# Two row pairs instead of one at each pass's end of a gated feed-forward block

## The chip, the cores and the metric

The kernel runs on one core of one Trainium2 chip. The metric is device time in microseconds of one execution; lower is better. Before the change the median of three runs is 1755.19 us (1753.89 to 1756.28).

## The reference: what is computed

One transformer block with an adaptive layer norm. Six vectors of 512 (shift, scale and gate for each half) come from a small product with a condition vector. The first half is attention: 2048 query rows, 32 heads of 128 that share 8 key and value heads, over the last 512 cached positions. The second half, where the change lies, is a gated feed-forward net with inner width 1792:

```
h = _layernorm(x) * (1 + cb) + sb
x = x + gb * ((_gelu(h @ w_gate) * (h @ w_up)) @ w_down)
```

Everything is float32 outside; x is 2048 x 512.

## The kernel before, in words

*Precision.* Each float32 operand is split into a high and a low float16 half, and a product is three matmuls of 128x128 by 128x512 (low by high, high by high, high by low), summed in one bank of PSUM. All go through the helper at line 89.

*Attention* takes most of the time. It is written as a list of 512 steps whose order on every engine is fixed by hand. In its second half the feed-forward weights are prepared between its steps: scaled, combined, split and stored in device memory under keys (tiles `stage`, `kept`), by `prep_set` for gate and up and by `prep_wd` for the down weights.

*The feed-forward part* goes twice over the inner width, once for each half of the 2048 rows (a pass). A pass has seven pairs n of two f-tiles (NP = 7, so n runs from 0 to 13 over both passes). For each pair there are two matrices, q = 2n (gate) and q = 2n + 1 (up), 28 in all. A matrix is a 2x2 block product by seven products instead of eight (Winograd's form of Strassen); the loop at the end of the kernel walks its seven products in the order 1, 2, 6, 7, 5, 4, 3. Each is six matmuls, and each is called a step here; it has the index k from 0 to 6. The sums go to banks of the names fa, fb, fc. ACT copies some of them out (fg, fu, u; line 884), DVE adds the others (line 1269), ACT applies the GELU with a scale (line 1275), DVE multiplies gate by up (line 1286), and ACT and DVE or POOL split the result into the halves `at` (lines 1296 and 1297).

*The down product* of a pair comes in two kinds, told apart by `turned(n)`:
- By rows (`y_tasks`): for each of the eight row tiles, two f-tiles, six matmuls. The bank is `py`, and DVE adds it to the row tile `acc` (line 951). 48 matmuls a pair.
- Turned (`yt_tasks`): seven products in each of two halves p of the model width, on four combinations of the activations that POOL makes (`sums_of`, lines 1302 and 1297). 42 matmuls a pair. The output is transposed: DVE adds each product into eight tiles `yt` of 128 columns by 512 rows (line 1655, or 1658 for the first).

Before, six of the seven pairs of a pass are turned and the last is by rows. At the end of a pass the eight `yt` tiles are turned back: ACT splits each into its upper and lower 16-bit parts (`yu`, line 1664), a transposing DMA on SP's queue writes `yv` (line 1669), ACT puts the parts together to rows `yr` (line 1685), and POOL adds them to `acc` (line 1686), which holds the first half's result reloaded from device memory. Then the row tile goes out (`f_final`).

*What sets the order.* Products of the down kind wait in a list `nexty`; `y_next` takes the first entry and issues it. `put_off(n, fn)` runs fn n steps later (`tick` counts one at each step). In the feed-forward part this order is the program's order; on PE, DVE, ACT and POOL a planner with its own costs sets the final order, taking the earliest instruction in the program that its model finds ready. SP's queue, which issues all these DMAs, stays in the order written: weight fetches for the next matrices (`set_fetch`, `wd_fetch`), the transposes, row loads and output stores stand behind one another.

*Buffers.* Tiles of one kind share a number of buffers: `p16` four (the splits yu, and fu, the up-matrix's first copy), `qt` three, `raw` five, `acc` eight (the `yt` tiles and the row tiles share them), `ot` twelve (the halves `at`), and five PSUM banks `acc` beside one `qa` and two `s`.

Of the kernel before, what the change touches and what calls it, by code (L numbers as in the profile page):

```python
# [12 lines left out]
U16 = mybir.dt.uint16  # L13
BF16 = mybir.dt.bfloat16
AF = mybir.ActivationFunctionType
ALU = mybir.AluOpType
AX = mybir.AxisListType

P = 128
# [3 lines left out]
KT = D // P  # L23
NF = F // P
NT = S // P
QB = 512
QT = QB // P
# [17 lines left out]
NRAW = 5  # L45
NRW = 2
NWR = 2
GW = 3
NACC = 5
NP16 = 4  # L50
# [13 lines left out]
def block_kernel(ctx: ExitStack, tc: tile.TileContext, x, kT, v, wq, wo, wg, wu, wd, cT, wc, wm, out):  # L64
    nc = tc.nc

    const = ctx.enter_context(tc.tile_pool(name="const", bufs=1))
    pool = ctx.enter_context(tc.tile_pool(name="pool", bufs=2))
# [7 lines left out]
    def raw(name):  # L76
        return pool.tile([P, 512], F32, tag="raw", name=name, bufs=NRAW)
# [13 lines left out]
    acc, moved, bg = {}, [0], []  # L91
# [9 lines left out]
    def rows_of(t, i):  # L101
        return t[i * P:(i + 1) * P, :]
# [188 lines left out]

    def turned(n):

        return n % NP < NP - 1

    def f_spread(i, m):
        w = little("lw", 1, 2)
# [157 lines left out]
    def put_off(n, fn):  # L455

        waits_.append([n, fn])
# [137 lines left out]
    for g in range(NG):  # L595
        half, pr = divmod(g, NPR)
        for j, qb in (PLAIN if g < GW else TURNED):
            units.append((half, pr, 2 * half + qb, 2 * pr + j))
# [194 lines left out]
    def set_steps(key, by, act=False):  # L793
        l, r = slice(0, 256), slice(256, 512)

        def tt(o, a, b, op):
            nc.gpsimd.tensor_tensor(o, a, b, op=op)

        def s0():
            SET[key] = [get_w(0)]  # L800
            times(RAW[key][0], by)
            halves(SET[key][0], RAW[key][0], act)

        def s1():
            r1 = RAW[key][1]
            times(r1, by)
            SET[key] += [None, None, pool.tile([P, 2, 256], F16, tag="x3", name="x3", bufs=2)]
            halves(SET[key][3], r1[:, r], act)
            tt(r1[:, r], r1[:, l], r1[:, r], ALU.add)

        def s2():
            r0, r1 = RAW[key][0], RAW[key][1]
            tt(r1[:, l], r0[:, l], r1[:, l], ALU.subtract)
            tt(r0[:, l], r1[:, r], r0[:, l], ALU.subtract)
            tt(r0[:, r], r0[:, r], r0[:, l], ALU.subtract)

        def s3():
            SET[key][1] = get_w(1)
            halves(SET[key][1], RAW[key][0], act)

        def s4():
            SET[key][2] = get_w(2)
            halves(SET[key][2], RAW[key].pop(1), act)

        return s0, s1, s2, s3, s4
# [22 lines left out]
    def sched_set(key, srcs, t0, by, spread):  # L848
        s0, s1, s2, s3, s4 = set_steps(key, by)
        a, b, c, d, e, f = SETPOS2 if key == GW else SETPOS  # L850
        sched_pair(key, srcs, t0 - a, spread, [(t0 - b, s0), (t0 - e, s3)], [(t0 - c, s1), (t0 - d, s2), (t0 - f, s4)])
# [357 lines left out]
    for g in range(NG):  # L1209
# [5 lines left out]
        spread = None if half else lambda m, pr=pr: w_spread(pr, m)  # L1215
        if 0 < g < GW:
            a, b = plain_steps(g, by)
            sched_pair(g, srcs, t0 - (19 if g > 1 else 13), spread, [(t0 - (13 if g > 1 else 8), a)], [(t0 - (11 if g > 1 else 7), b)])
        elif g >= GW and (not half or pr < GW):
            sched_set(g, srcs, t0, by, spread)  # L1220
            if not half:
                a, b, c, d, e, f = SETPOS2 if g == GW else SETPOS
                for k, pos in ((0, t0 - b + 4), (3, t0 - c + 4), (1, t0 - e + 4), (2, t0 - f + 4)):
# [27 lines left out]
    NP = NF // 2  # L1251
    NQ = 4 * NP
# [134 lines left out]
    def prep_wd(n, b):  # L1387
# [4 lines left out]
        def load(k):  # L1392
            st[k] = pool.tile([P, D], F32, tag="wr", name="wr", bufs=NWR)
            dma(st[k], wd[(2 * n + k) * P:(2 * n + k + 1) * P, :])
# [72 lines left out]
    loads.sort(key=lambda l: l[0])  # L1467
    released = {"raw": [0] * NRAW, "rw": [0] * NRW, "wr": [0] * NWR}
    for pos, (load, steps), kind, ahead in loads:
# [38 lines left out]
    def pushes(u, y):  # L1508
        g, k = divmod(u, 4)
        pv = pv_tasks(u - 2) if 2 <= u < NU + 2 else []  # L1510
        if u >= NU:
# [6 lines left out]
            return []  # L1518
        nxt = items(g + 1) if g + 1 >= GW else None
        if g < GW:  # L1520
# [14 lines left out]
    with tc.manual_schedule():  # L1535
        begin()
        nexty, invs = [], {}
        for t in range(T + TAIL):
            now[0] = t
            u, s = divmod(t, 4)  # L1540
# [65 lines left out]
    def y_next():  # L1606
        if nexty:
            all_of(nexty.pop(0))
# [15 lines left out]
    for i in range(2 * QT):  # L1624
        q = 7 * (2 + i // 2) + 3 * (i % 2)
        load, norm, split, turn = ln_turned(i)
# [6 lines left out]
    for p in range(2):  # L1633
        q = 51 + 14 * p
# [4 lines left out]

    def f_final(ti):  # L1640
        assert ti in back
        if ti not in halfway:
            return halfway.add(ti)
        if ti >= 2 * QT:
            dma(rows_of(out, ti), acc[ti])
        else:
            put_off(2, lambda: dma(rows_of(out, ti), acc[ti]))

    YT, YR, back, halfway = {}, {}, set(), set()

    def yt_add(n, c, qb, ps):
        by = ST["dyc"][:, KT * (n % NP) + c:KT * (n % NP) + c + 1]
# [7 lines left out]
    def yt_turn(g, c, qb):  # L1660

        def split():
            u = YR["u", c, qb] = pool.tile([P, 2, QB], U16, tag="p16", name="yu", bufs=NP16)
            nc.scalar.activation(u, YT[g, c, qb].bitcast(U16).rearrange("p (r h) -> p h r", h=2), AF.Copy)

        def turn():
            if ("t", qb) not in YR:
                YR["t", qb] = pool.tile([P, KT, 2 * QT, P], U16, tag="pt", name="yv", bufs=NPT)
            nc.sync.dma_start_transpose(YR["t", qb][:, c], YR.pop(("u", c, qb)).rearrange("p a b -> p (a b)"))

        split()
        put_off(2, turn)
        YR["n"] = YR.get("n", 0) + 1
        if YR["n"] % QT == 0:
            for i in range(QT):
                ti = 2 * QT * g + (YR["n"] - 1) % (2 * QT) // QT * QT + i
                put_off(3, lambda ti=ti: load_acc(ti, y1[ti]) or back.add(ti))

    def yt_rows(g, qb):
        t = YR.pop(("t", qb)).rearrange("p c (h i) q -> p c q h i", h=2)  # L1680
        for i in range(QT):
            ti = 2 * QT * g + QT * qb + i
            assert ti in back
            r = raw("yr")
            nc.scalar.activation(r.bitcast(U16).rearrange("p (c q h) -> p c q h", c=KT, h=2), t[:, :, :, :, i], AF.Copy)
            nc.gpsimd.tensor_tensor(acc[ti], acc[ti], r, op=ALU.add)
            f_final(ti)

    ADDS = {1: ((0, 0),), 2: ((0, 0),), 6: ((0, 1),), 5: ((1, 1),), 7: ((1, 1),), 4: ((1, 0),), 3: ((0, 1),)}
    YORDER = (1, 2, 6, 5, 7, 3, 4)  # L1690
    LAST = {2: (0, 0), 7: (1, 1), 3: (0, 1), 4: (1, 0)}

    def yt_tasks(n):
        tasks = []
        for p in range(2):
            st = {}
            bk = banks(st, {"a": ("acc", "ya", NACC) if p else ("qa", "ya", 1), "b": ("acc", "yb", NACC), "c": ("acc", "yc", NACC)})

            def group(k, p=p, bk=bk):
                a, b = PROD[k]  # L1700
                x, start = CHAIN[k]
                ci, off = YCOL[a]
                w, t = WO["f", n, ci], A[n, {"b11": "11", "b21": "21", "b22": "22"}.get(b, b)]
                sl = slice(off + p * P, off + (p + 1) * P)
                mm3(bk(x)(), w[:, 0, sl], w[:, 1, sl], t[:, 0, :], t[:, 1, :], start, k in (2, 4, 3), True)

            def post(k, p=p, st=st):
                (i, qb), = ADDS[k]
                yt_add(n, 2 * i + p, qb, st[CHAIN[k][0]])
                if n % NP == NP - 2 and k in LAST:  # L1710
                    i, qb = LAST[k]
                    c, g = 2 * i + p, n // NP
                    put_off(1, lambda: yt_turn(g, c, qb))
                    if p and k in (3, 4):
                        put_off(7 if g else 9, lambda: yt_rows(g, qb))

            tasks += [[(lambda k=k, f=group: f(k), lambda k=k, f=post: f(k))] for k in YORDER]
        return tasks

    YCOL = {"a11": (0, 0), "a12": (0, 256), "s2": (1, 0), "s3": (1, 256), "s4": (2, 0), "s1": (2, 256), "a22": (3, 0)}  # L1720

# [1 line left out]
    for q in range(NQ):  # L1723
        n, m = divmod(q, 2)
        its = items(NG + q) if q < 2 else f_items(q)
        for k, pk in enumerate(ORDER):
            if (q, pk) not in f_done:
                all_of(its[pk])
            run(("f", q, k))
            tick()  # L1730
            if n and k == 2 and m == 0 and turned(n - 1):
                nexty += yt_tasks(n - 1)
            if k in ((1, 2, 5, 6) if q < NQ - 1 else (1, 5)) or (n and turned(n - 1)):
                y_next()
            if q == NQ - 2 and k > 1 or (q, k) in ((NQ - 1, 1), (NQ - 1, 2)):
                y_next()
        if m == 1 and not turned(n):
            for qi, (a, b) in enumerate((("11", "21"), ("12", "22"))):
                for i in range(QT):
                    nexty.append(y_tasks((2 * (n // NP) + qi) * QT + i, [lambda n=n, a=a: A[n, a], lambda n=n, b=b: A[n, b]],  # L1740
                                         [("f", n, 0), ("f", n, 1)], col("dysc", n % NP), f_final))
# [40 lines left out]
```

## Time and profile before

| | us |
|---|---|
| median of three runs | 1755.19 |
| profiled execution | 1756.2 |
| its span, first to last instruction | 1754.4 |
| PE busy | 1713.0 (98%) |
| DVE busy | 1424.3 (81%) |
| ACT busy | 1263.0 (72%) |
| POOL busy | 1069.8 (61%) |

A row of a group gives line, engine, operation, output and inputs, shape and count, then the busy time, the mean in ns and the idle time of the engine before them with what ended it. A row of waits gives who waited for whom, the total, how often, and the longest. A row of the timeline gives start, duration, engine, what, and in brackets the idle time before. Busy times of PE overlap, since matmuls are pipelined: one is shown with some 380 ns, and the next one starts 216 ns after it.

### The profile page before, as it was taken

How to read it: one execution, taken by the hardware profiler on the slowest of the kernel's cores; microseconds unless marked ns; L12 is line 12 of the kernel's file. 1: busy time of each engine (PE TensorE's matmuls, PEld its weight loads, DVE VectorE, ACT ScalarE, POOL GpSimd, SP SyncE). 2: the span in 40 equal slices, each digit the busy share in tenths (PEclk: the TensorE clock that was granted, in tenths of full speed). 3: DMA queues.
4: the chain of work that ended last, by engine and by line, in shares of the span. 5: the costliest groups of instructions: out<-in, count | busy, mean ns of one | idle time of the engine just before them, and what ended most of it. 6: DMA issues, size and time to landing. Idle time of an engine off the chain costs nothing.

```text
span 1754.4 us, 26202 instructions
## 1 busy us (share of the span) xinstructions
PE 1713.0 (98%) x8008; PEld 785.4 (45%) x8010; DVE 1424.3 (81%) x2464; ACT 1263.0 (72%) x2819; POOL 1069.8 (61%) x1292
## 2 busy tenths in 40 slices
PE   7999999999999999999999999999999999999995
PEld 5444444444444444444444444444444444444442
DVE  7898898888888899888888888888885687747764
ACT  6988888888878777887778777787773744553334
POOL 4889777776888874655585585675511657243342
PEclk9999999999999999999999999999999999999998
DMA  7999999999999999999999999999985663463325
GB/s 236 217 206 210 212 215 210 223 206 219 222 209 235 202 210 178 216 208 235 202 213 230 215 212 212 205 220 218 204 169 146 190 190 105 117 208 117 100 84 150
DMA packets 691885, 341.01 MB, mean 194 GB/s; under 512 B 578976, under 2 KB 602272, under 8 KB 691744
## 3 DMA queue, kind: packets, MB, share of 16 engines
q1 hardware_dynamic: 691456, 338.81, 84.8%
q8 instruction: 63, 1.03, 0.3%
q14 instruction: 78, 0.64, 0.1%
q10 hardware_dynamic: 288, 0.52, 0.1%
HBM read 136.45 MB, written 62.26 MB: 113 GB/s over the span
## 4 chain that ended last, share of the span: by engine, by line
PE 81%; DVE 5%; ACT 5%; DMA 3%; POOL 3%; issue 2%; SPq 0%; DVEq 0%; POOLq 0%; ACTq 0%
PE py L89 18%; PE po L89 16%; PE ps L89 16%; PE qa L89 8%; PE fa L89 6%; PE qc L89 4%; PE fc L89 3%; PE ya L89 2%; PE qb L89 2%; PE fb L89 2%; PE yc L89 1%; DMA pt<-p 1%; ACT ee L990 1%; ACT p L1002 1%; PE pq L89 1%
## 5 line engine op out<-in xcount | busy, mean ns | idle before, releaser
L990 ACT ACTIVATE ee<-ps,nm 128x512 f32<-128x512 f32 x512 | 349.8, 683 | 191.9 <-DVE nm L981 188.2
L1007 DVE SCALAR_TENSOR_TENSOR p<-ee,rr,p 128x512 f16<-128x512 f32 x512 | 456.4, 891 | 5.0 <-ACT p L1002 4.2
L981 DVE TENSOR_REDUCE nm<-ps 128x1 f32<-128x512 f32 x512 | 350.4, 684 | 104.7 <-PE ps L89 101.9
L89 PE MATMUL ps<-k,qt 128*128 128x512 f16 x1536 | 415.1, 379 | 6.1 <-ACT ee L990 5.1
L1002 ACT ACTIVATE p<-ee,rr 128x512 f16<-128x512 f32 x512 | 364.4, 712 | 20.8 <-DVE rr L998 10.5
L89 PE MATMUL po<-pt,v 128*128 128x512 f16 x1536 | 373.1, 380 | 2.2 <-DMA pt<-p 2.1
L89 PE MATMUL py<-wo,ot 128*128 128x512 f16 x1536 | 371.5, 380 | 0.0
L89 PEld LDWEIGHTS <-w 128*128 128x128 f16 x2184 | 213.0, 98 | 267.2 <-issue 7.0
L89 PEld LDWEIGHTS <-v 128*128 128x128 f16 x1536 | 149.8, 98 | 184.6 <-issue 2.5
L89 PEld LDWEIGHTS <-ot 128*128 128x128 f16 x1536 | 150.1, 98 | 181.7 <-DVE ot L739 0.4
L89 PEld LDWEIGHTS <-qt 128*128 128x128 f16 x1536 | 145.8, 98 | 177.5 <-issue 4.6
L1302 POOL TENSOR_TENSOR fg<-fg 128x512 f32<-128x512 f32 x48 | 62.3, 1299 | 142.4 <-DVE fg L1286 141.4
L739 DVE SCALAR_TENSOR_TENSOR ot<-po,ot 128x512 f16<-128x512 f32 x128 | 87.7, 685 | 39.4 <-ACT ot L738 39.1
L1296 ACT ACTIVATE at<-fg 128x512 f16<-128x512 f32 x92 | 56.9, 625 | 66.8 <-DVE fg L1286 40.0
L990 ACT ACTIVATION_READ_ACCUMULATOR ee<-ps,nm 128x1 f32 x512 | 100.0, 195 | 0.0
L951 DVE SCALAR_TENSOR_TENSOR acc<-py,ysc,acc 128x512 f32<-128x512 f32 x128 | 94.7, 740 | 6.2 <-PE py L89 6.2
L234 POOL TENSOR_TENSOR lw<-lw,half__86 128x1 f32<-128x1 f32 x37 | 23.4, 631 | 104.9 <-DVE lw L184 104.8
L89 PE MATMUL fa<-t,w 128*128 128x512 f16 x336 | 82.7, 379 | 4.2 <-ACT u L884 2.2
L89 PE MATMUL qa<-t,w 128*128 128x512 f16 x348 | 84.9, 380 | 0.0
L396 POOL TENSOR_TENSOR rs<-rs,nhalf 128x1 f32<-128x1 f32 x32 | 18.7, 584 | 102.6 <-DVE rs L390 99.7
L1655 DVE SCALAR_TENSOR_TENSOR yt<-ya,dyc,yt 128x512 f32<-128x512 f32 x84 | 61.8, 745 | 23.9 <-PE ya L89 23.5
L89 PE MATMUL ya<-at,wo 128*128 128x512 f16 x288 | 77.5, 379 | 1.5 <-ACT at L1296 0.9
(241 smaller groups left out, 2802.3 us busy)
## 6 DMA issues: line engine op xcount, KB each, us to landing
w<-kept SPq DMA_DIRECT2D x123, 256.0 KB, 3.3
wo<-kept SPq DMA_DIRECT2D x72, 256.0 KB, 3.3
kept<-stage SPq DMA_DIRECT2D x62, 256.0 KB, 3.2
raw<-in_wo SPq DMA_DIRECT2D x56, 256.0 KB, 3.3
kept<-w SPq DMA_DIRECT2D x39, 256.0 KB, 3.5
rw<-in_wq SPq DMA_DIRECT2D x38, 256.0 KB, 3.2
hs<-hf SPq DMA_DIRECT2D x32, 256.0 KB, 2.8
pt<-p SPq DMA_TRANSPOSE x512, 3.5
```

The costliest lines, as they stand in the source:

```text
L89: nc.tensor.matmul(ps, a, b, start=first and n == 0, stop=last and n == 2, skip_group_check=chain)
L234: nc.gpsimd.tensor_tensor(out, out, half_, op=ALU.pow)
L396: nc.gpsimd.tensor_tensor(st["rs"], st["rs"], nhalf, op=ALU.pow)
L739: return lambda: nc.vector.scalar_tensor_tensor(t[:, 1, :], src, scale, t[:, 0, :], op0=ALU.mult, op1=ALU.subtract)
L951: nc.vector.scalar_tensor_tensor(acc[ti], st["p"], by, acc[ti], op0=ALU.mult, op1=ALU.add)
L981: nc.vector.tensor_reduce(nm, E[t]["ps"], axis=AX.X, op=ALU.max, negate=True)
L990: nc.scalar.activation(e, E[t]["ps"], AF.Exp, bias=E[t]["nm"], scale=1.0, accum_out=sm[:, t % 2:t % 2 + 1])
L1002: nc.scalar.activation(p16[:, 0, :], E[t]["e"], AF.Copy, scale=E[t]["r"])
L1007: nc.vector.scalar_tensor_tensor(p16[:, 1, :], E[t]["e"], E[t]["r"], p16[:, 0, :], op0=ALU.mult, op1=ALU.subtract)
L1296: nc.scalar.activation(t[:, 0, :], g, AF.Copy)
L1302: nc.gpsimd.tensor_tensor(g[o], g[a], g[b], op=ALU.subtract)
L1655: nc.vector.scalar_tensor_tensor(YT[key], ps, by, YT[key], op0=ALU.mult, op1=ALU.add)
```

## The change

`NROW = 2` pairs at each pass's end are by rows instead of one, so five of seven are turned. The preparation of the down weights follows `turned(n)`. The turned products are put into the list two by two, and taken at steps k = 1, 2, 5 and 6 alone, where before one was taken at every step (two at some steps of the last two matrices). Splits take buffers of the kind `qt` instead of `p16`; their transposes are issued three steps behind the split instead of two; the split of two of the eight tiles is put off one step more. The row copies and POOL's adds are put off one by one instead of four in one call: 9 to 12 steps after the last product for rows of the first block of 512, and 13 to 16 for the second, where before it was 9 (first pass) or 7 (second). A row tile is final after three contributions instead of two.

```diff
+NROW = 2
     def turned(n):
 
-        return n % NP < NP - 1
+        return n % NP < NP - NROW
...
     def f_final(ti):
         assert ti in back
-        if ti not in halfway:
-            return halfway.add(ti)
+        halfway[ti] = halfway.get(ti, 0) + 1
+        if halfway[ti] <= NROW:
+            return
...
-            u = YR["u", c, qb] = pool.tile([P, 2, QB], U16, tag="p16", name="yu", bufs=NP16)
+            u = YR["u", c, qb] = pool.tile([P, 2, QB], U16, tag="qt", name="yu", bufs=3)
...
-        put_off(2, turn)
+        put_off(3, turn)
...
-    def yt_rows(g, qb):
-        t = YR.pop(("t", qb)).rearrange("p c (h i) q -> p c q h i", h=2)
-        for i in range(QT):
-            ti = 2 * QT * g + QT * qb + i
-            assert ti in back
-            r = raw("yr")
-            nc.scalar.activation(r.bitcast(U16).rearrange("p (c q h) -> p c q h", c=KT, h=2), t[:, :, :, :, i], AF.Copy)
-            nc.gpsimd.tensor_tensor(acc[ti], acc[ti], r, op=ALU.add)
-            f_final(ti)
+    def yt_row(g, qb, i):
+        t = YR["t", qb].rearrange("p c (h i) q -> p c q h i", h=2)
+        ti = 2 * QT * g + QT * qb + i
+        assert ti in back
+        r = raw("yr")
+        nc.scalar.activation(r.bitcast(U16).rearrange("p (c q h) -> p c q h", c=KT, h=2), t[:, :, :, :, i], AF.Copy)
+        nc.gpsimd.tensor_tensor(acc[ti], acc[ti], r, op=ALU.add)
+        f_final(ti)
+        if i == QT - 1:
+            del YR["t", qb]
...
-                if n % NP == NP - 2 and k in LAST:
+                if n % NP == NP - NROW - 1 and k in LAST:
                     i, qb = LAST[k]
                     c, g = 2 * i + p, n // NP
-                    put_off(1, lambda: yt_turn(g, c, qb))
+                    put_off(2 if k in (3, 4) and p == k // 4 else 1, lambda: yt_turn(g, c, qb))
                     if p and k in (3, 4):
-                        put_off(7 if g else 9, lambda: yt_rows(g, qb))
-
-            tasks += [[(lambda k=k, f=group: f(k), lambda k=k, f=post: f(k))] for k in YORDER]
-        return tasks
+                        for r in range(QT):
+                            put_off((9 if k == 4 else 13) + r, lambda r=r: yt_row(g, qb, r))
+
+            tasks += [(lambda k=k, f=group: f(k), lambda k=k, f=post: f(k)) for k in YORDER]
+        return [tasks[k:k + 2] for k in range(0, len(tasks), 2)]
...
-            if k in ((1, 2, 5, 6) if q < NQ - 1 else (1, 5)) or (n and turned(n - 1)):
-                y_next()
-            if q == NQ - 2 and k > 1 or (q, k) in ((NQ - 1, 1), (NQ - 1, 2)):
+            if k in ((1, 2, 5, 6) if q < NQ - 1 else (1, 5)):
                 y_next()
```

More of the change, by code (lines that the diff above doesn't have):

```diff
@@ L1647, in f_final @@
             put_off(2, lambda: dma(rows_of(out, ti), acc[ti]))
-    YT, YR, back, halfway = {}, {}, set(), set()
+    YT, YR, back, halfway = {}, {}, set(), {}
     def yt_add(n, c, qb, ps):
```

## The prediction

> **What bounds the kernel now.** I read the page first, then the list of waits of PE, then the chain, ACT's and SP's rows of the two places where PE waits, last the granted clock.
>
> ```profile
> PE 1713.0 (98%) x8008; PEld 785.4 (45%) x8010; DVE 1424.3 (81%) x2464; ACT 1263.0 (72%) x2819; POOL 1069.8 (61%) x1292
> PE   7999999999999999999999999999999999999995
> ```
>
> The reader is to see that PE is the bound from the second slice to the last but one, and that only the last slice (43.9 us) is half empty for it. So a change after the attention can do two things: add or remove matmuls at the full price of PE, and fill the holes of PE. These are the holes from 1480 us to the end, first the window 1700 to 1755, then the one from 1480 to 1700.
>
> ```profile
> PE py L89 <- ACT at L1296: 5.3, 2, 4.8
> PE fa L89 <- ACT u L884: 2.2, 1, 2.2
> PE fa L89 <- ACT fu L884: 1.9, 1, 1.9
> PE ya L89 <- DVE yt L1655: 0.6, 1, 0.6
> PE fc L89 <- DVE fg L1269: 0.3, 1, 0.3
> PE yc L89 <- ACT at L1296: 0.2, 1, 0.2
> ...
> PE fa L89 <- DMA w<-kept: 1.9, 1, 1.9
> ```
>
> The second list has one line: the end of the first pass costs PE 1.9 us. The end of the second pass costs 5.3 + 2.2 + 1.9 + 0.6 + 0.3 + 0.2 = 10.5 us. After the longest wait the clock drops as well (windows; columns: engine busy times, then granted clock):
>
> ```profile
> 1720.00:1733.00 13.00, 9.56 (x43) 4.11 (x43) 6.83 (x10) 7.41 (x11) 0.00 (x0) 1.00 1.11 249
> 1733.00:1739.00 6.00, 1.29 (x6) 0.39 (x4) 2.11 (x4) 5.90 (x7) 3.27 (x3) 0.84 0.61 189
> 1739.00:1744.00 5.00, 4.91 (x12) 1.80 (x13) 0.92 (x1) 3.23 (x4) 5.00 (x5) 0.51 0.14 52
> ```
>
> Two pieces of the chain give the pace of a matmul at full clock, and what the last products cost:
>
> ```profile
> 1694.42 2.59 PE fa L89 x12
> ...
> 1739.09 7.73 PE py L89 x24
> ```
>
> Twelve matmuls take 2.59 us, 0.216 us each. The last 24 should have taken 5.18 us and took 7.73: 2.55 us lost at the granted clock of 0.51. So the end holds 10.5 + 2.55 = 13.05 us of lost PE time, the first pass's end 1.9 us.
>
> Why PE waits there is in ACT's rows near the end:
>
> ```profile
> 1717.23 2.95 ACT L1664 ACTIVATE yu<-yt 128x1024 uint16<-128x1024 uint16 x3 [2.57 <-DVE yt L1655]
> 1720.09 0.57 ACT L884 ACTIVATE fu<-fa 128x512 f32<-128x512 f32 x1
> ...
> 1733.10 5.42 ACT L1685 ACTIVATE yr<-yv 128x1024 uint16<-128x1024 uint16 x5 [1.62 <-DMA yv<-yu]
> 1738.42 0.61 ACT L1296 ACTIVATE at<-fg 128x512 f16<-128x512 f32 x1
> ...
> 1542.85 5.43 ACT L1685 ACTIVATE yr<-yv 128x1024 uint16<-128x1024 uint16 x5 [0.59 <-DMA yv<-yu]
> ```
>
> All is the turning back of the transposed sums. The splits (yu) take a buffer of the p16 kind, of which fu takes one too, and give it back only when a transpose has landed; they stand on ACT ahead of the copies fu and u that free PE's bank. Then five row copies (yr) in one piece, 5.42 us, stand ahead of the copy at that the last row products read. The last row is the same piece at the end of the first pass. The transposes wait in SP's queue, and in the first pass weight fetches stand between them:
>
> ```profile
> 1536.12 1.83 SPq L1669 DMA_TRANSPOSE yv<-yu  x1
> 1538.04 1.00 SPq L95 DMA_DIRECT2D w<-kept  x2
> 1539.14 2.67 SPq L1669 DMA_TRANSPOSE yv<-yu  x2
> ...
> yv<-yu SPq DMA_TRANSPOSE x8, 3.3
> ...
> 1747.27 1.41 DVE L951 SCALAR_TENSOR_TENSOR acc<-py,dysc,acc 128x512 f32<-128x512 f32 x2 [0.46 <-PE py L89]
> ...
> 1748.70 2.39 SPq L95 DMA_DIRECT2D out_y<-acc  x5
> ```
>
> The last two of these rows are the tail behind PE: two adds in one piece, then five output transfers in one piece.
>
> **The change part by part.** The prices of what moves, from the groups of 1200 us to the end:
>
> ```profile
> L1655 DVE SCALAR_TENSOR_TENSOR yt<-ya,dyc,yt 128x512 f32<-128x512 f32 x84 | 61.8, 745 | 23.9 <-PE ya L89 23.5
> L1296 ACT ACTIVATE at<-fg 128x512 f16<-128x512 f32 x92 | 56.9, 625 | 66.8 <-DVE fg L1286 40.0 <-POOL fg L1302 26.7
> L1297 DVE TENSOR_TENSOR at<-fg,at 128x512 f16<-128x512 f32 x44 | 35.6, 816 | 15.5 <-ACT at L1296 15.2
> L1286 DVE SCALAR_TENSOR_TENSOR fg<-fg,gsc,u 128x512 f32<-128x512 f32 x28 | 23.3, 831 | 0.1
> L1686 POOL TENSOR_TENSOR acc<-acc,yr 128x512 f32<-128x512 f32 x16 | 20.6, 1322 | 57.9 <-DMA acc<-y 57.9
> L1685 ACT ACTIVATE yr<-yv 128x1024 uint16<-128x1024 uint16 x16 | 17.6, 1161 | 2.2 <-DMA yv<-yu 2.2
> L1664 ACT ACTIVATE yu<-yt 128x1024 uint16<-128x1024 uint16 x16 | 16.2, 1049 | 8.6 <-DVE yt L1655 7.5 <-DMA yv<-yu 1.1
> ```
>
> *One more pair by rows in each pass.* Seven products in two halves are 42 matmuls; eight row tiles of six are 48. Two passes: 12 more, 12 x 0.216 = 2.6 us, on the path since PE is the bound. Off the path, each pair saves POOL four differences and four subtractions, ACT three copies (3 x 0.625 = 1.9 us), DVE 14 sums against 8 row adds of the same kind (6 x 0.745 = 4.5 us) and gains one subtraction (0.82). Also two fewer weight tiles are stored once and fetched in each pass. I cost these at nothing: PE at 98% covers them, and were the cover gone they would be gains.
>
> *Its weights by rows.* In the attention the preparation of pair 5 issues two stores for four and fewer POOL steps, and takes two fewer staging buffers, so later loads may start earlier. PE shows no hole that hangs on it; zero, with half a microsecond either way from the size of the holes of 0.2 to 0.6 us listed above.
>
> *Turning back, earlier and spread.* The last seven-product pair is now followed by two pairs of rows. The last transposed product of a pass stood in the third step of the last up-matrix; it now stands in the last step of the matrix two before it, 2 x 7 steps earlier than the end. The work to be turned is the same: 8 x 1.05 us of splits, 8 x 1.16 us of row copies, 8 x 1.32 us on POOL, eight transposes. Beside it run two f-matrices of 7 x 6 matmuls each and eight row products of six, 132 matmuls or 28.5 us of PE in the window between, of which ACT needs 8.4 + 9.3 = 17.7 us for the turning; its own f-work in these two matrices is six copies like fu (6 x 0.57), four copies at (4 x 0.625) and four GELUs, 5.9 us beside the GELUs. It fits without a full queue. The 10.5 us of waits and the 2.55 us of slow clock then have no cause: 13.05 us gained.
>
> *Buffers and SP.* The splits move from the p16 kind to the three buffers of the qt kind, which in this part only the turned inputs use, and those are done early. So fu no longer waits for a transpose. A split needs the buffer of the split three before it; the design puts at least three steps between a split and its transpose's issue, and a transpose lands 3.3 us after issue, so the fourth split, more than three steps (3 x 1.29 us) and one slot of products after the first, should find its buffer free. On SP each transpose stands three steps instead of two behind its split, so SP does not stand at it, and the weight fetches behind it go on time: the 1.9 us of the first pass go. The row loads (four issues behind the fourth and the eighth split) stand three steps behind theirs as before. SP's issues are the same in number there, less two wo fetches a pass.
>
> *Row copies one a step.* They are written nine to sixteen steps later. On ACT and POOL the planner sets the order, and it will take them as soon as its model has the transposes landed (in the first pass it ran five together in front of their place, too). What is late next is one ACT wait for a transpose, as the 1.62 us of the row at 1733.10. I take 1.6 us as lost in the second pass, with nothing in the first, whose piece of five cost PE nothing; bounds 0 and 7.35 us (the old hole of 4.8 with its slow clock of 2.55).
>
> *Products two at a time.* Seven calls in four steps of each matrix instead of fourteen in every step; the matmuls are the same. The order on PE and DVE is the planner's, which fills a wait with other products. Taken at 0; bounds in the rivals.
>
> *The tail.* Row adds come one by one at 1.29 us, so the last add waits for no other (1.41 - 0.745 = 0.67 us less) and its transfer is not the fifth of a piece (four fifths of 2.39: 1.9 us less). Gain 2.6 us; bounds 0 and 3.05 (both pieces gone, 3.80 us, but for one add).
>
> Sum: 13.05 + 1.9 + 2.6 - 2.6 - 1.6 = 13.35 us faster. The profiled execution took 1756.2 us with a span of 1754.4 us; it lies 1.0 us over the median of 1755.2 us. Against the median: 1741.9 us.
>
> On the clock, the rows show that holes of 2.2 and 1.9 us left it at 1.00 and the one of 4.8 us brought 0.51. The Trainium skill, TensorE: Matmul & The Clock Gate, Part 1, says that an idle window of about 3.4 us halves the clock and about 3.4 us of steady work restore it. By that figure alone the slow stretch would have cost about 1.7 us and not 2.55, and the estimate would be 1742.8 us; the row decides.
>
> **The rivals.**
>
> *The planner bunches the row copies again (partial gain).* For it: both passes of before show five copies in one piece though written to follow products. If at for the last rows stands behind them once more, 4.8 + 2.55 = 7.35 us come back in place of the 1.6: gain 13.35 + 1.6 - 7.35 = 7.6 us, 1747.6 us. Against it: the copies now become ready a whole matrix before the last at, and six row tiles of products (36 matmuls, 7.8 us) lie between the last up-product and the rows that need it (two of pair 12's, four of pair 13's), against a chain of an add (counted like a sum, 0.745), scaling 0.83, copy 0.625 and subtraction 0.82, together 3.0 us.
>
> *Two products at a time make PE wait for DVE (slower).* Place: the up-matrix of each pair during which transposed products run. There 6' follows 1' on the same bank after one f-product and 2' (1.29 + 0.65 us), and 3' follows 5' after 7' and one f-product. Between, DVE has the add, scaling and subtraction of that step and two sums (3 x 0.745 + 0.83 + 0.82 = 3.9 us) and the copy on ACT (0.625): 4.5 us behind the f-product's end, when PE wants it at 3.25 us; so 1.3 us a pair at the first place. At the second two f-products have handed DVE their steps (2 x (0.83 + 0.625 + 0.82) + 2 x 0.745 = 6.0 us behind the first one's end), when PE wants it at 3.9 us (3 x 1.29): 2.1 us. Were the order as written, ten such pairs would give 34 us. It decides above 13.35 / 10 = 1.3 us a pair; at half its price 17 us are lost and it ends at 1759 us. Against it: from 1480 to 1700 us PE has only the one wait for weights, so the planner's order hides such chains today.
>
> *The turning is not what ends the pass.* If the holes only move to the last row products for lack of work between, the gain is the 1.9 + 2.6 alone against 2.6: 1753.3 us. The 36 matmuls speak against it.
>
> **How the numbers follow.** Forecast 60% (its own range 1738 to 1745), bunched copies 20% (1745 to 1752), slower by pairs 14%, holes moved 6%. The range 1737.5 to 1752 holds the first two; below it goes to no residual wait and the whole tail (13.05 + 1.9 + 3.05 - 2.6 = 15.4 us), the half microsecond of the attention, and one hole of 1.5 us in the middle of a pass that another order may close:
>
> ```profile
> PE fa L89 <- ACT fg L884: 1.5, 1, 1.5
> ```
>
> Together 17.4 us. Anything within 0.2% (3.5 us), about what a measurement of this kernel can tell, counts as same. Faster: 60 + 20 and part of the last, 82%; same 4%; slower 14%.
>
> **What would show it.** PE with 8020 matmuls; 140 transposed sums for 168; 32 row adds with the pair's scale for 16. ACT's yu rows with no wait for yv; no wait of PE above 1 us after 1480 us; the clock at 1.00 to the last matmul; out_y issues one by one. Wrong: PE waiting for yt at L1655 in the middle of a pass, yr rows in a piece of five just ahead of at, or w<-kept late at a pass's end.

## The result and the profile after

| | before | after |
|---|---|---|
| median, us | 1754.74 | 1745.17 |
| lowest to highest, us | 1753.89 to 1756.28 | 1743.57 to 1745.53 |
| span of the profiled execution, us | 1754.4 | 1741.8 |
| from the last matmul's end to the span's end, us | 7.6 | 4.0 |

Both medians are of four runs; the four of before are the three known ahead of the prediction and one more, so their median is 1754.74 and no longer 1755.19. The ratio is 0.9943 with a 95% interval of 0.9926 to 0.996: 9.6 us faster by the medians, 7 to 13 by the interval. The forecast was 13.35 us, to 1741.9; the measured 1745.17 lies in the range of 1737.5 to 1752 and 0.2 us above the forecast's own range of 1738 to 1745. Repeated beside three variants, the same kernel gave 0.9938 (0.9924 to 0.9951) and 1744.87 us. The spans of the two profiled executions differ by 12.6 us, 3 more than the medians: the profile of before was taken 1.5 us above its median (1756.2), and that of after is its fastest run (1743.57), 1.6 us below.

The page's line of PE, and the waits of PE, first in the window 1480 to 1700 and then from 1700 us to the end, in the kernel after (its lines are one or two further down than before):

```profile
PE 1714.7 (98%) x8022; PEld 787.0 (45%) x8022; DVE 1417.6 (81%) x2454; ACT 1258.5 (72%) x2813; POOL 1045.9 (60%) x1266
```

```profile
PE fa L90 <- ACT fu L885: 0.3, 1, 0.3
...
PE fa L90 <- ACT u L885: 1.4, 2, 0.7
PE fc L90 <- DMA w<-kept: 0.9, 1, 0.9
PE py L90 <- ACT at L1297: 0.4, 2, 0.2
PE fc L90 <- DVE fg L1270: 0.2, 1, 0.2
```

The end's waits fell from 10.5 us to 2.9, none is above 1 us, and the first pass's 1.9 us for weights went (0.3 us for fu is there in its place). The window from 1700 us to the last matmul has the clock at 1.00:

```profile
1700.00:1738.00 38.00, 34.72 (x154) 14.37 (x151) 19.81 (x30) 18.73 (x23) 10.30 (x8) 1.00 0.59 165
```

The turning itself is not smooth. ACT's rows near the end:

```profile
1698.69 2.94 ACT L1666 ACTIVATE yu<-yt 128x1024 uint16<-128x1024 uint16 x3
1702.90 1.06 ACT L1666 ACTIVATE yu<-yt 128x1024 uint16<-128x1024 uint16 x1 [1.27 <-DMA yv<-yu]
...
1707.87 1.06 ACT L1666 ACTIVATE yu<-yt 128x1024 uint16<-128x1024 uint16 x1 [3.09 <-DMA yv<-yu]
...
1714.42 5.43 ACT L1686 ACTIVATE yr<-yv 128x1024 uint16<-128x1024 uint16 x5 [3.21 <-DMA yv<-yu]
1719.75 0.61 ACT L1297 ACTIVATE at<-fg 128x512 f16<-128x512 f32 x1
```

Two splits wait for a buffer, 4.4 us together, and the row copies come five in one piece behind a wait of 3.2 us, as before. What differs is PE's side. While ACT makes the row copies, PE goes through the last 18 row products of the first row pair, which need nothing of the turning:

```profile
1714.90 1.24 PE L90 MATMUL py<-wo,at 128*128 128x512 f16 x5
...
1717.27 2.97 PE L90 MATMUL py<-wo,at 128*128 128x512 f16 x13
```

SP shows where the transposes are late:

```profile
1696.27 4.72 SPq L1671 DMA_TRANSPOSE yv<-yu  x2
1701.09 1.95 SPq L96 DMA_DIRECT2D acc<-y  x4
1703.13 1.23 SPq L1671 DMA_TRANSPOSE yv<-yu  x1
1704.42 0.57 SPq L96 DMA_DIRECT2D w<-kept  x1
1705.08 0.42 SPq L96 DMA_DIRECT2D x<-kept  x1
1705.60 1.46 SPq L1671 DMA_TRANSPOSE yv<-yu  x1
1707.16 0.53 SPq L96 DMA_DIRECT2D w<-kept  x1
1707.78 1.23 SPq L1671 DMA_TRANSPOSE yv<-yu  x1
1709.06 0.58 SPq L96 DMA_DIRECT2D w<-kept  x1
1709.73 1.23 SPq L1671 DMA_TRANSPOSE yv<-yu  x1
1711.02 2.53 SPq L96 DMA_DIRECT2D acc<-y  x4
1713.59 0.91 SPq L96 DMA_DIRECT2D wo<-kept  x2
1732.19 6.79 SPq L96 DMA_DIRECT2D out_y<-acc  x8
```

In the first row SP issues one transpose and then stands for the next one's split. From 1701.09 to 1714.50 us it then issues without a pause: the rows there add up to 12.6 us of 13.4. The splits wait for the transposes' buffers, the transposes for their turn on SP. The last row is the outputs, issued as the adds finish; SP ends 1.2 us behind the last matmul, where before five were still to be issued.

### The profile page after: what moved, and what is told of

It reads as the page before. It is cut to its first block, busy times and chain, and to the rows that moved or that the text cites. A ratio compares the mean times of both kernels' runs of the same rounds, so it can differ in the third digit from the quotient of the medians.

```text
span 1741.8 us, 26188 instructions
## 1 busy us (share of the span) xinstructions
PE 1714.7 (98%) x8022; PEld 787.0 (45%) x8022; DVE 1417.6 (81%) x2454; ACT 1258.5 (72%) x2813; POOL 1045.9 (60%) x1266
## 4 chain that ended last, share of the span: by engine, by line
PE 82%; ACT 5%; DVE 5%; DMA 3%; POOL 2%; issue 2%; SPq 0%; ACTq 0%; DVEq 0%; POOLq 0%
PE py L90 19%; PE ps L90 17%; PE po L90 17%; PE qa L90 8%; PE fa L90 6%; PE qc L90 4%; PE fc L90 3%; PE ya L90 2%; PE qb L90 2%; PE fb L90 2%; PE yc L90 1%; ACT ee L991 1%; DMA yv<-yu 1%; ACT p L1003 1%; DVE nm L982 1%
## 5 line engine op out<-in xcount | busy, mean ns | idle before, releaser
L1303 POOL TENSOR_TENSOR fg<-fg 128x512 f32<-128x512 f32 x40 | 51.8, 1295 | 135.6 <-DVE fg L1287 103.0
L1297 ACT ACTIVATE at<-fg 128x512 f16<-128x512 f32 x86 | 53.4, 625 | 64.8 <-DVE fg L1287 44.5
L739 ACT ACTIVATE ot<-po 128x512 f16<-128x512 f32 x128 | 73.8, 577 | 5.0 <-PE po L90 5.0
L1657 DVE SCALAR_TENSOR_TENSOR yt<-ya,dyc,yt 128x512 f32<-128x512 f32 x68 | 50.1, 745 | 22.1 <-PE ya L90 21.7
```

The costliest lines, as they stand in the source:

```text
L739: nc.scalar.activation(t[:, 0, :], src, AF.Copy, scale=scale)
L1297: nc.scalar.activation(t[:, 0, :], g, AF.Copy)
L1303: nc.gpsimd.tensor_tensor(g[o], g[a], g[b], op=ALU.subtract)
L1657: nc.vector.scalar_tensor_tensor(YT[key], ps, by, YT[key], op0=ALU.mult, op1=ALU.add)
```

## The experiments

All were timed beside the kernel before, which had a median of 1755.4 to 1756.0 us. Each ratio has an interval of some 2 us either way, so differences of 1 or 2 us between variants are not shown. Waits, windows and rows are of one profiled execution of each kernel.

**The change again.**

> The changed kernel itself, in the same company as the next three. Holes theory (the gain is PE's holes at the pass's end, filled by row products, against 12 more matmuls at 2.6 us): 9 to 11 us faster than before, about 1745 us. No rival differs here; it is the mark for the others.

Measured: 1744.87 us, ratio 0.9938 (0.9924 to 0.9951). Its profile has a little more of the same holes than the one above: 4.5 us of PE waits from 1480 us on, against 3.2.

```profile
PE fa L90 <- ACT u L885: 1.4, 2, 0.7
PE fc L90 <- DVE fg L1270: 1.2, 1, 1.2
PE fa L90 <- ACT fu L885: 0.9, 1, 0.9
PE fc L90 <- DMA w<-kept: 0.6, 1, 0.6
PE py L90 <- ACT at L1297: 0.4, 2, 0.2
```

Below, "the change" is this run.

**The second row pair alone.** The kernel before with

```diff
-        return n % NP < NP - 1
+        return n % NP < NP - NROW
...
-            if q == NQ - 2 and k > 1 or (q, k) in ((NQ - 1, 1), (NQ - 1, 2)):
-                y_next()
```

and the counts in `f_final` and `yt_tasks` that go with it.

> The kernel before with the second row pair alone: products one at a time, splits in the p16 buffers, transposes two steps behind, four row copies in one call. Holes theory: most of the gain, 6 to 9 us faster than before, since the row products stand behind the turning whatever its form; waits of PE at the end below 7 us in sum. Rival (spreading and buffers make the gain, the row pair is only a cost): 2 to 3 us slower than before.

Measured: 1746.68 us, ratio 0.9945 (0.9933 to 0.9958), 8.8 us faster. The holes theory holds. The interval overlaps that of the change, so it is not shown that the rest of the change adds anything to the second row pair. The waits of PE that are left from 1480 us on are others:

```profile
PE fa L90 <- DMA w<-kept: 5.0, 4, 1.6
PE py L90 <- ACT at L1297: 0.5, 1, 0.5
```

Without the later transposes and the own buffers it is the weight fetches behind the transposes that are late.

**Spreading and buffers alone.** The changed kernel with `NROW = 1`, and extra calls at four steps of the last two matrices:

```diff
-NROW = 2
+NROW = 1
...
+            if (q, k) in ((NQ - 2, 3), (NQ - 2, 4), (NQ - 1, 0), (NQ - 1, 2)):
+                y_next()
```

> The changed kernel with one row pair a pass (NROW = 1) and four extra calls in the last two matrices, so that the products are out in time; all else as changed. Rival (spreading and buffers): 1740 to 1745 us, better than the change by its 2.6 us of matmuls. Holes theory: at most 3 us faster than before, since nothing but eight row tiles stands behind the turning; PE again waits over 3 us at a time and the clock drops.

Measured: 1749.5 us, ratio 0.9965 (0.9953 to 0.9978), 6.0 us faster. It fell between the two expectations: spreading is worth more than the holes theory gave it, and still 4.6 us less than the whole change, although it has 12 matmuls fewer. Its 6.0 us and the 8.8 us of the row pair alone cannot be added (the change gains 10.7): both remove the same holes. Its waits of PE from 1480 us on sum to only 5.8 us:

```profile
PE py L90 <- ACT at L1297: 3.0, 1, 3.0
PE py L90 <- DMA wo<-kept: 1.1, 1, 1.1
PE ya L90 <- ACT at L1297: 0.9, 1, 0.9
PE fa L90 <- DMA w<-kept: 0.8, 2, 0.6
```

The longest is 3.0 us again, and behind it the clock falls, as the holes theory expected:

```profile
1728.00:1734.00 6.00, 4.24 (x10) 1.37 (x11) 1.47 (x3) 1.63 (x2) 0.00 (x0) 0.50 1.13 228
```

Ten matmuls in 4.24 us, which take 2.2 us at 0.216 us each, are about 2 us lost. The rest went to the tail. POOL's row, then SP's:

```profile
1736.05 9.83 POOL L1687 TENSOR_TENSOR acc<-acc,yr 128x512 f32<-128x512 f32 x8 [28.38 <-ACT yr L1686]
```

```profile
1737.35 8.89 SPq L96 DMA_DIRECT2D out_y<-acc  x8
```

POOL adds the turned rows until 1745.9 us, and SP issues outputs until 1746.2, while the last matmul ends at 1740.1: the tail is 8.7 us. In the change the tail is 4.1 us. So the second row pair takes away the long hole with its slow clock, and moves the chain of row copies, adds and outputs off the end.

**Products one at a time.**

```diff
-        return [tasks[k:k + 2] for k in range(0, len(tasks), 2)]
+        return [[t] for t in tasks]
...
-            if k in ((1, 2, 5, 6) if q < NQ - 1 else (1, 5)):
+            if k in ((1, 2, 5, 6) if q < NQ - 1 else (1, 5)) or (n and turned(n - 1)):
```

> The changed kernel with the transposed products one at a time, one at every step, as before. Rival (two at a time makes PE wait for DVE): 3 us or more faster than the change, with fewer waits of PE in the middle of the passes. Holes theory with the planner's order: within 1.5 us of the change.

Measured: 1745.14 us, ratio 0.9938 (0.9925 to 0.995). It is the change's time: within the noise, two at a time neither costs nor gains. The waits of PE in the middle of the passes (1200 to 1480 us) did not get fewer either: 2.9 us here, 2.3 in the change.

**The kernel before without turning in the second pass.**

```diff
-        split()
-        put_off(2, turn)
+        if g == 0:
+            split()
+            put_off(2, turn)
...
-                    if p and k in (3, 4):
+                    if p and k in (3, 4) and g == 0:
```

and a row tile of the second pass is final one contribution sooner. The kernel no longer computes the whole result; it is there for its time alone.

> The kernel before with the second pass's turning left out (no splits, transposes, row copies and POOL adds there; the row tiles are still loaded, and the transposed sums of the second pass are computed but not used). Holes theory (turning makes the end's waits, the slow clock and the longer tail): 13 us of holes and about 3.5 us of tail go, 1737 to 1741 us. Rival (the end waits for lack of independent products whatever is turned): 1748 us or more.

Measured: 1738.29 us, ratio 0.9903 (0.9889 to 0.9916): 17.1 us less than the kernel before (1755.43 beside it). PE's only wait from 1480 us on is at the first pass's end:

```profile
PE fa L89 <- DMA w<-kept: 1.5, 1, 1.5
```

The granted clock shows no slow stretch before the last matmul, and the tail is 4.3 us. So the whole end, with the slow clock and 3.3 us of the tail, hangs on the turning.

**The changed kernel without turning in the second pass**, by the same edit.

> The changed kernel with the second pass's turning left out in the same way. What is left of the turning's cost: holes theory 3 to 5 us, so 1740 to 1742 us; rival (turning is now hidden whole): within 1.5 us of the change, 1743.5 to 1746.

Measured: 1741.19 us, ratio 0.992 (0.9907 to 0.9934), 3.7 us less than the change. PE's waits from 1480 us on are 0.9 us here and 4.5 in the change, and the tail is as long (4.0 and 4.1 us), so the profiles put these 3.7 us into holes of PE. Together with the run above: turning at the end cost 17.1 us and costs 3.7, and the two kernels without it differ by 2.9 us, which is the 2.6 us of the 12 matmuls and 0.3 for everything else, the first pass's end included. These three differences add up to the 10.6 us between the medians of the change and of before because they are taken from the same four medians; they divide the gain and do not confirm it. The profile does: from before to the run without turning PE's waits fall from 12.4 to 1.5 us, 2.55 us of slow clock go and 3.3 us of tail, 16.8 us of the 17.1.

**Five buffers for the splits.**

```diff
-            u = YR["u", c, qb] = pool.tile([P, 2, QB], U16, tag="qt", name="yu", bufs=3)
+            u = YR["u", c, qb] = pool.tile([P, 2, QB], U16, tag=("qt", "v16")[YR.get("n", 0) % 8 in (1, 3, 6)], name="yu", bufs=(3, NV16)[YR.get("n", 0) % 8 in (1, 3, 6)])
```

> The changed kernel with five buffers for the splits (three of the kind qt and two of the kind v16). If ACT's 4.4 us of waits for a split's buffer make the holes that are left: 1 to 3 us faster than the change, 1742 to 1744 us, and no wait of yu for yv. Rival (the transposes stand in SP's queue behind weight fetches, whatever the buffers): within 1 us of the change, ACT's wait moves to yr.

Measured: 1744.14 us, ratio 0.9937 (0.9924 to 0.9951): the change's time. No split waits any more, and nothing is gained. The last transpose on SP, then the last splits and the piece of row copies on ACT:

```profile
1709.89 1.23 SPq L1671 DMA_TRANSPOSE yv<-yu  x1
```

```profile
1698.82 2.94 ACT L1666 ACTIVATE yu<-yt 128x1024 uint16<-128x1024 uint16 x3
...
1714.55 5.43 ACT L1686 ACTIVATE yr<-yv 128x1024 uint16<-128x1024 uint16 x5 [3.29 <-issue]
```

The splits are done at 1701.8 us, 7 us earlier than with three buffers in the profile of after, but the last transpose and the row copies start within 0.2 us of where they did there. It is SP's queue and not the buffers that holds the last transpose back: its split had been done for 8 us.

**Transposes one step behind their splits.**

```diff
-        put_off(3, turn)
+        put_off(1, turn)
```

> The changed kernel with each transpose one step behind its split on SP's queue instead of three, ahead of the weight fetches of the steps between. If these fetches hold the transposes up: yu's and yr's waits for yv fall from 4.4 and 3.2 us, and the time by 1 to 2 us. Rival (the weight fetches become late behind the transposes, as with rows alone): waits of PE for w of 2 us and more, and 1 to 3 us slower than the change.

Measured: 1745.7 us, ratio 0.9946 (0.9934 to 0.9959). Both halves came true at once in the profile, and the time is the change's within the noise. The row copies hardly wait any more, but a weight fetch is late and the clock falls (waits of PE and ACT, then a window):

```profile
PE fa L90 <- DMA w<-kept: 3.6, 2, 3.2
...
ACT yr L1686 <- DMA yv<-yu: 0.2, 1, 0.2
```

```profile
1697.00:1703.00 6.00, 5.76 (x14) 2.11 (x15) 1.05 (x2) 3.78 (x5) 0.00 (x0) 0.51 1.08 248
```

**The same with earlier weight fetches.**

```diff
-        for k, at_ in ((0, 2), (3, 2), (1, 3), (2, 4)):
+        for k, at_ in ((0, 2), (3, 2), (1, 3), (2, 4)) if q % 14 not in (12, 13) else ((0, 0), (3, 0), (1, 1), (2, 1)):
...
-        put_off(3, turn)
+        put_off(1, turn)
```

> Transposes one step behind their splits as in the last run, and the weight fetches of the last two matrices of each pass (q = 12, 13, 26, 27) two steps earlier in SP's order, ahead of the transposes. If SP's order is what sets the holes that are left: no wait of PE for w above 0.5 us, none of yr for yv, clock 1.00, 2 to 3.5 us faster than the change: 1741.5 to 1743 us. Rival (the row copies in one piece on ACT set the holes): within 1 us of the change, 1744 to 1746 us.

Measured: 1744.31 us, ratio 0.9929 (0.9917 to 0.9942). It is the lowest ratio of all that compute the whole, but the interval overlaps that of the change, so it is not shown to be better. The time is the rival's (1744 to 1746). The waits for w went, as expected. The row copies' wait did not:

```profile
PE py L90 <- ACT at L1297: 2.0, 2, 1.8
...
ACT yr L1686 <- DMA yv<-yu: 4.3, 1, 4.3
```

The 1.8 us are the rival's place: the copy `at` that ends this wait stands on ACT right behind the five row copies (from 1716.8 to 1722.2 us). These copies waited in their turn for the transposes, the last two of which SP issued from 1709.5 to 1713.5 us, one of them in 2.48 us, twice the usual 1.23; why is not known.

**And with five buffers too.**

> The same with five buffers for the splits. If a split still waits for a buffer there (1.1 us of ACT with one step and three buffers): up to 0.7 us faster than without; else the same within 0.7 us.

Measured: 1746.12 us, ratio 0.9939 (0.9926 to 0.9951): no gain, and 1.8 us above the run without, outside what was expected, though the intervals overlap. In its profile (the slowest of its runs) a fetch is late again by 2.0 us, and the clock falls behind that hole:

```profile
PE fa L90 <- DMA w<-kept: 2.6, 2, 2.0
```

```profile
1713.00:1717.00 4.00, 4.00 (x12) 1.47 (x11) 0.52 (x1) 1.32 (x2) 0.00 (x0) 0.58 1.27 262
```

**Row copies on DVE.**

```diff
-        nc.scalar.activation(r.bitcast(U16).rearrange("p (c q h) -> p c q h", c=KT, h=2), t[:, :, :, :, i], AF.Copy)
+        nc.vector.tensor_copy(r.bitcast(U16).rearrange("p (c q h) -> p c q h", c=KT, h=2), t[:, :, :, :, i])
```

> The changed kernel with the row copies yr on DVE instead of ACT. If the piece of five copies on ACT makes the holes that are left (copies u and at behind it): 1 to 2.5 us faster than the change. Rival (whichever engine has the copies stands still for the transposes, and DVE feeds PE too): the same within 1 us or slower, with waits of PE for DVE in place of ACT.

Measured: 1752.11 us, ratio 0.9979 (0.997 to 0.9988): 7.2 us slower than the change, more than the rival gave. A copy takes DVE as long as ACT (1.18 and 1.17 us), DVE stands still for the transposes in the same way, and PE now waits for DVE:

```profile
PE py L90 <- DVE acc L952: 3.4, 3, 2.1
PE fa L90 <- ACT u L885: 2.0, 1, 2.0
PE py L90 <- DVE fu L1270: 1.6, 1, 1.6
```

**Three row pairs.** `NROW = 3`.

> The changed kernel with three pairs by rows in each pass (NROW = 3), four turned. 12 more matmuls at 0.216 us cost 2.6 us. If what is left of the turning (3.7 us in the second pass by the run that left it out) comes from too little work behind it, a third pair hides it: up to 1 us faster than the change, 1743.5 to 1745 us. Rival (the transposes land late wherever they stand, and ACT waits for them with the same holes): 2 to 3 us slower, 1747 to 1748 us, with holes of PE of some 4 us around the turning.

Measured: 1747.53 us, ratio 0.9951 (0.9937 to 0.9965), with single times from 1745.38 to 1750.16. The median is in the rival's range, the mechanism isn't the rival's. In the profile (the slowest of these runs) PE has no listed wait at all from 1600 us to the end: a third pair does hide the second pass's turning. The profile's loss is at the first pass's end, where a weight fetch came late and the clock fell:

```profile
PE fa L90 <- DMA w<-kept: 3.3, 1, 3.3
```

```profile
1491.00:1497.00 6.00, 5.94 (x15) 2.19 (x16) 1.22 (x2) 2.16 (x4) 0.00 (x0) 0.52 1.21 245
```

That stretch is not what sets the median: only the two slowest runs have the lower mean clock (0.998), and the three at 1.00 took 1745.38, 1746.51 and 1747.53 us. That is 0.5 to 2.7 us above the change, of which the 12 matmuls make 2.6, and the interval overlaps the change's; a loss beyond these matmuls is not shown. In the profile the waits from 1200 to 1480 us are longer too (4.9 us, against 2.3 in the change); whether the faster runs share them is open.

Three pairs in the second pass alone were not tried; they would need the down weights prepared in two forms.

## Why the prediction was right, and where its sizes were off

The time is in the range, and the mechanism held in its main part: work put behind the turning fills the holes of PE. Two of the steps by which the size was worked out failed, and one of the prediction's own signs of being wrong appeared, a piece of five row copies just ahead of `at`. Of the other signs, the counts came out (140 transposed sums, 32 row adds with the pair's scale, 8020 matmuls in the repeated run), the clock stayed at 1.00 and the outputs went out one by one; the splits did wait for transposes.

*The bound and the holes.* Right. PE is the bound, and the 13 us of waits and slow clock at the end were the turning's: without turning the kernel before ends 17.1 us sooner, which is the 13.05 us and the tail's 3.3, with 0.7 us left over.

*Twelve more matmuls at 2.6 us.* It fits: 2.9 us between the two kernels without turning, 8020 matmuls in the repeated run. The weights by rows, taken at 0 in the attention, show nothing there: its last matmuls (`po`) start at 1337.4 us before and at 1337.2 after.

*What is late next.* This is one of two terms that were mis-sized: 1.6 us were taken, 3.7 were measured. Half of the place was right. In the change's list above, the waits behind the second pass's turning come to 3.6 us (all but the 0.9 for fu, which is in the first pass). Of the 1.4 us for u and the 0.4 for at, 0.9 us stand on ACT directly behind the row copies, which came late, five in one piece and then three; the rest follows in the same chain of copies and products. The other half was not foreseen: 0.6 us for a late weight fetch, and 1.2 for a sum fg that DVE makes only after a row add, which had waited 1.3 us for its row to be loaded:

```profile
1707.28 0.75 DVE L952 SCALAR_TENSOR_TENSOR acc<-py,dysc,acc 128x512 f32<-128x512 f32 x1 [1.26 <-DMA acc<-y]
```

Row loads and weight fetches come from SP. "SP does not stand at it" is the step that failed. SP did stand, for a split, in the 4.72 us of two transposes, and then had to issue eight loads, four transposes and six fetches behind one another. Issues that were costed as the same in number were not costed in time: 1.23 us for a transpose and about 0.5 for a load, in the very stretch in which the row copies wait. That a split finds its buffer free failed with it: two splits waited 4.4 us together. Three steps behind the split put the transposes behind the fetches of those steps; one step (the eighth run) put the fetches behind the transposes. Five buffers show that the splits' waits were no cause by themselves.

*The first pass.* 1.9 us were expected to go. This is the other mis-sized term. In the differences above next to nothing is left for it: 0.3 us beside the 2.6 of the matmuls, and of the wrong sign, which is within the noise of these medians. The profile of after shows the hole gone (0.3 us for 1.9; 0.9 in the repeated run), and the waits between 1270 and 1480 us did not take its place: they fell from 3.0 to 1.9 us, though one of 0.8 us for weights is new. Why the medians show nothing of it isn't settled.

*The tail.* 2.6 us were taken, with a bound of 3.05; it went from 7.6 to 4.0 us, 3.6. SP issues the last output 1.2 us behind the last matmul, where it was 4.3 us before; an output takes the same from issue to landing (median 2.2 us in both profiles).

*Together*: 13.35 less 2.1 (what is late next) and less 1.9 (first pass) plus 1.0 (tail) is 10.35 us; the two comparisons gave 9.6 and 10.7. Since these corrections are themselves measured on the same runs, this is no second test.

*Two products at a time.* Taken at 0, measured at 0.3 us, which is nothing within the noise. The rival's 34 us had the order on DVE as written. That the planner's order is what avoids it was argued and not tested; the 3.25 us in its price are also given without their terms.

*Bunched copies.* The planner did bunch them, five in 5.43 us ahead of at, as the rival said, and yet the price of 7.35 us was not paid: 18 row matmuls, 3.9 us, ran meanwhile. This is what the row pair is for, and the run with one row pair shows it from the other side: 3.0 us of PE waiting for at. So the rival's forecast time (1747.6) was missed by 2.4 us although what it foresaw on ACT happened.

*The clock.* Gone with the long hole, as forecast. The prediction went by a hole's length. The Trainium skill, TensorE: Matmul & The Clock Gate, Part 1, has the window in which activity is counted free-running, so where a hole falls in it would matter beside its length. The runs fit that: a hole of 2.2 us left the clock at 1.00 in the kernel before, one of 2.0 us brought 0.58 in the tenth run. That the position is the reason is not shown. Both 2.0 us there and the 3.0 us with one row pair are below the 3.4 us that the prediction cites from the same part, and they brought the slow clock all the same; here the measurement decides.

## What to carry to other kernels

Where the end of a pass hangs on a long chain over several engines, put independent work behind the chain's start and not only space into it: the extra row pair cost 2.6 us and was worth more than the spreading by itself (8.8 us against 6.0), although five of eight row copies still came in one piece. When a transfer is moved in an in-order queue, add up the issue times of everything in that stretch, since a queue that never waits can still be late. And a planner that takes whatever its model finds ready undoes spreading that is only written into the order.

## What the runs showed that was not expected

A transposing transfer holds SP for 1.23 us at the least, against some 0.4 to 0.6 for the plain ones in the rows above. In the second pass of the kernel after it landed 3.1 to 5.2 us after its issue (median 4.1); the prediction used the median of before, 3.3 (3.1 to 5.3). A late weight fetch of 3.2 us costs nearly twice its length: in the eighth run's window behind the hole, 6 us at a clock of 0.51, 14 matmuls ran, which take 3.0 us at 0.216 us each.
